# One table of single steps for the start of a pooled-attention and maxout kernel

## The chip, the cores and the metric

The kernel runs on one core of a Trainium2 chip. The metric is the device time of one execution in microseconds; a time given for a kernel is the median of several executions. The engines are named as in the profile: PE (TensorE), DVE (VectorE), ACT (ScalarE), POOL (GpSimd) and SP (SyncE, which here only issues transfers). Each executes its own instructions in the order in which the program gives them.

## The reference

Four batches of 12288 queries attend to 768 keys each. The keys are averages of 4x4 patches of `kv`, projected by `w_sr`, and they are the values too. The result, 49152 rows of 128, goes through a maxout layer with three matrices and an output matrix.

```python
kv_pool = kv.reshape(B, H // 4, 4, W // 4, 4, C).mean(axis=(2, 4))   # B=4, H=384, W=32, C=128
k = v = kv_pool.reshape(B, -1, C) @ w_sr                             # 768 keys for each batch
s = (1 / np.sqrt(C)) * (q @ k.transpose(0, 2, 1))                    # q: (4, 12288, 128)
a = np.exp(s - s.max(-1, keepdims=True))
a /= a.sum(-1, keepdims=True) + 1e-09
x = (a @ v).reshape(B * N, C)
h = np.maximum(np.maximum(x @ w1, x @ w2), x @ w3)                   # w: (128, 768), float64
out = (h @ w_out).astype(np.float32)                                 # w_out: (768, 128), float64
```

## The kernel before

The queries are cut into 96 groups (`NG`) of 512 rows, and a group into four tiles of 128. Nearly every matmul operand is split into two float16 parts, a high and a low one, scaled by powers of two, and three products of the parts stand for one. So for a group PE does:

- four score tiles (`scores`, token S): six matmuls of 128x384 each, into one of two double banks `ps_s`;
- the attention (`attend`, token X, in two halves of nine matmuls), from the softmax weights that a DMA transpose has turned into `aT`;
- six hidden blocks (`hidden`, token H): three matmuls of 128x512 for `w2 - w1` and three for `w3 - w1`, into the two banks `ps_h`. With `w1` taken off beforehand the maximum of three becomes a maximum with zero, and what `w1` itself adds comes back through one product of `w1` and `w_out` (`product_w1`, `w1o`);
- six projections (`project`, token O), three matmuls each and three more with `w1o` for the last block.

Around a score tile, DVE takes the maximum (`soft_max`, m, tiles `mx` and `nb`), ACT the exponential (`soft_exp`, e, tile `a`) and the cast to float16 (`soft_hi`, c), POOL the remainder (`soft_lo`, l, tile `ahl`), and SP issues the transpose to `aT`. Around a hidden block, ACT does a relu (R), DVE the maximum with the second product (M, tile `h`), ACT the cast (C, `hh`) and POOL the remainder (L, `hl`). `attended_hi` and `attended_lo` (xh, xl) split the attention's result; the q tokens load (qd), scale (qc), measure (qp), and split (qh, ql) the queries.

The order is written out by hand. A wrapper (`InOrder`) keeps each engine's instructions in the order of the program. From the first hidden block on, the strings of `ORDER`, twelve of them for the six blocks of an even and an odd group, say in which order the tokens' steps are issued. A token takes all that has come due (`drain`).

What stands before that is a straight list of calls. It loads `w_sr`, the twelve pieces of the first batch's `kv` (512 KB each) and the first queries; it sums the patches with DVE adds, folds and PE products with the identity (`gather`), projects and splits the keys; then come the weights. The weights arrive as 64-bit floats. `Weights64` makes a 32-bit float of each value: it clamps the upper word's magnitude (`clamp`), shifts it left by three (`shift`), adds three bits of the lower word (`low`) and the sign (`sign`); then `w1` is taken off (`rest`), the peak is found (`top`), and two float16 parts are made (`split_hi` on ACT, `split_lo` on DVE). Four matrices in two halves make eight such objects; their steps form a list `todo`, and `more(n)` issues the next n of them at chosen places, between the softmax steps of the groups 0 and 1 and, through `late`, between their hidden blocks. In the first half the clamp runs as an Abs on ACT and a max-min on POOL, in the others as a mask and a max-min on DVE. The buffers of `kvp`, 13 of 512 KB, hold both the pieces of `kv` and the raw weights.

Of the kernel before, what the change touches and what calls it, by code (L numbers as in the profile page):

```python
# [20 lines left out]
def kernel(  # L21
# [34 lines left out]
    R = 4  # L56
# [76 lines left out]
    col = const.tile([C, 1], F32, name="col")  # L133
    d_top = const.tile([P, 2, 4], F32, name="d_top")
# [15 lines left out]
    FIRST = (1, 1, 1, 1, 0, 1, 1, 1, 1, 2, 0, 1)  # L150
    LEFT = (12, 12, 12, 12, 12)
    LO_ON_DVE, HI_ON_DVE, HL_ON_DVE = ((), (6, 8), ())
    OUT_AT, OUT_ON = (1, 8), ("dve", "dve")
    ATTEND = {0: (4, 4), 1: (4, 4)}
    LATE = (1,)
    W_LOW, W_HIGH = 2.0 ** -15 * 1.125, 122879.9921875
# [15 lines left out]
    OUTS = {2: (), 3: (), 4: (0, 1, 2)}  # L172

    def sr_weights():
        e = prep.tile([C, C], F32, name="sr_e")
        dve.tensor_scalar(
            out=e.bitcast(I32), in0=wsr_sb.bitcast(I32), scalar1=0x7FFFFFFF, scalar2=None, op0=ALU.bitwise_and
        )
        ps = spare(True)
        mm(out=ps[:, :C], lhsT=ones, rhs=e, start=True, stop=True)  # L180
        pow2(col_row, ps[:, :C])
        dve.reciprocal(out=e, in_=col_row)
        dve.tensor_tensor(out=wsr_sb, in0=wsr_sb, in1=e, op=ALU.mult)
# [20 lines left out]
    class Weights64:  # L204
# [7 lines left out]
        def __init__(self, n, w, h, hi, lo, wide=False):  # L212
            self.n, self.h, self.wide, self.w = n, h, wide, w
            self.lay = (lambda t: t.rearrange("p (t c) -> p t c", c=C)) if wide else lambda t: t
            self.hi, self.lo = hi, lo
# [16 lines left out]
        def shift(self):  # L232
            dve.tensor_scalar(
                out=self.e.bitcast(I32), in0=self.e.bitcast(I32), scalar1=3, scalar2=0x3FFFFFF8,
# [18 lines left out]
        def rest(self, on=pool):  # L253
            on.tensor_tensor(out=self.e, in0=self.e, in1=W[0, self.h].e, op=ALU.subtract)
# [14 lines left out]
    def size_d(h):  # L269
        top = d_top[:, h]  # L270
        dve.tensor_reduce(out=top[:, 3:4], in_=top[:, :3], axis=AX.X, op=ALU.max)
        times(top[:, 3:4], top[:, 3:4], col)
        W["ps"] = spare(True)
        mm(out=W["ps"][:, :1], lhsT=ones, rhs=top[:, 3:4], start=True, stop=True)

    def sized_d(h):
        pow2(d_size[h], W.pop("ps")[:, :1], SMALL, LARGE)
# [46 lines left out]
    class Keys:  # L324


        def __init__(self, b):
# [3 lines left out]
            self.acc = {}  # L331
# [3 lines left out]
            self.top = tiny.tile([1, 1], F32, name="pool_top", bufs=2)  # L335
# [24 lines left out]
        def fold(self, s, i, n):  # L360

            view = self.pieces[s, i].rearrange("p (u j c) -> p u j c", u=KU, c=C)
            dve.tensor_tensor(out=view[:, :, :n], in0=view[:, :, :n], in1=view[:, :, n:2 * n], op=ALU.add)

        def gather(self, s, i, n, first, last):
# [4 lines left out]
            for u in range(KU):  # L370
# [13 lines left out]
        def gathered_size(self):  # L384
            self.turn_tops(True)
            self.tops()
            self.size(True)
            self.sized()

        def gathered_project(self, s):  # L390
            if s == 0:
                self.kps = (ps_x.tile([P, G], F32, name="ps_x"), ps_o.tile([P, NJ, C], F32, name="ps_o"))
            out = self.kps[1].rearrange("p j c -> p (j c)") if s == KS - 1 else self.kps[0][:, s * PW:]
# [5 lines left out]
        def gathered_hi(self, n):  # L399
            ps, ks = ((self.kps[0], slice(0, G)), (self.kps[1].rearrange("p j c -> p (j c)")[:, :PW], slice(G, NK)))[n]  # L400
            act.mul(out=self.k_hi[:, ks], in_=ps, mul=self.up)

        def gathered_lo(self, n):
            ps, ks = ((self.kps[0], slice(0, G)), (self.kps[1].rearrange("p j c -> p (j c)")[:, :PW], slice(G, NK)))[n]
# [26 lines left out]
        def turn_tops(self, first=False):  # L431
            self.tops_ps = spare(first)
            dve.tensor_reduce(out=self.m[:, KS:KS + 1], in_=self.m[:, :KS], axis=AX.X, op=ALU.max)
            mm(out=self.tops_ps[:1, :P], lhsT=self.m[:, KS:KS + 1], rhs=ident, start=True, stop=True)

        def tops(self):
            dve.tensor_reduce(out=self.top, in_=self.tops_ps[:1, :P], axis=AX.X, op=ALU.max)

        def size(self, first=False):
            self.size_ps = spare(first)  # L440
            mm(out=self.size_ps[:, :1], lhsT=ones[:1], rhs=self.top, start=True, stop=True)

        def sized(self):
            ps = self.size_ps[:, :1]
            dve.tensor_scalar(
                out=self.g.bitcast(I32), in0=ps.bitcast(I32), scalar1=EXPO, scalar2=None, op0=ALU.bitwise_and
# [24 lines left out]
        def values(self):  # L471
            sp_dma.dma_start_transpose(out=self.v_hi, in_=self.k_hi)
            sp_dma.dma_start_transpose(out=self.v_lo, in_=self.k_lo)
# [16 lines left out]
    def q_cols(g):  # L490
        t = q_half(g)
        pool.tensor_tensor(out=t, in0=t, in1=col_row.unsqueeze(1).to_broadcast([P, NJ, C]), op=ALU.mult)

    def q_peak(s):
# [3 lines left out]
        dve.tensor_reduce(out=row, in_=st["q"][s], axis=AX.XY, op=ALU.max, apply_absolute_value=True)  # L498
# [170 lines left out]
    def hidden_lo(g, f):  # L669
        h, hh = st["h"][g, f]  # L670
        hl = hp.tile([P, G], F16, name="hl", bufs=HB_)
        (dve if g * NFT + f in HL_ON_DVE else pool).tensor_tensor(out=hl, in0=h, in1=hh, op=ALU.subtract)
# [134 lines left out]
    def made(i, h, clamp_on=dve):  # L807
        w = W[i, h]
        return [lambda: w.clamp(clamp_on), w.shift, w.low, w.sign]

    def halves(h, clamp_on=dve, rest_on=pool):
        rests = [lambda i=i: W[i, h].rest(rest_on) for i in (1, 2)]
        return [
            *made(0, h, clamp_on), *made(1, h, clamp_on), rests[0], *made(2, h, clamp_on), rests[1],
            W[0, h].top, W[1, h].top, W[2, h].top, lambda: size_d(h),
        ]

    def splits(h):
        return [
            lambda: sized_d(h), W[1, h].split_hi, W[2, h].split_hi, W[1, h].split_lo, W[2, h].split_lo,  # L820
        ]

    first, second = halves(0, pool), halves(1)
    todo = [
        *first, *second[:2], *splits(0), *second[2:], *made(3, 0)[:2], *splits(1), *made(3, 0)[2:],
        W[3, 0].top, ratio_u, *made(3, 1), W[3, 1].top, size_u, sized_u,
        *(f for h in range(2) for f in (W[3, h].split_hi, W[3, h].split_lo)),
    ]

    def more(n):  # L830
        for _ in range(min(n, len(todo))):
            todo.pop(0)()

# [5 lines left out]
    k = KT[0] = Keys(0)  # L839
    for i in range(R):  # L840
        k.load(0, i)
    q_load(0)
    for s in range(1, KS):
        for i in range(R):
            k.load(s, i)

    sr_weights()
    k.gather(0, 0, R, True, False)
    k.gather(0, 1, R, False, False)
    k.add(0, 2, 3)  # L850
    k.gather(0, 2, R, False, True)
    q_cols(0)
    q_cols(1)
    k.gathered(0)
    q_peak(0)
    q_hi(0)
    q_hi(1)
    k.gather(1, 0, R, True, False)
    k.gathered_project(0)
    k.gathered_peak(0)  # L860
    k.add(1, 1, 2)
    q_lo(0)
    W[0, 0].load()
    q_lo(1)
    for w in ((1, 0), (2, 0), (0, 1), (1, 1), (2, 1), (3, 0), (3, 1)):
        W[w].load()
    k.gather(1, 1, R, False, False)
    k.gather(1, 3, R, False, True)
    k.gathered(1)
    k.add(2, 0, 1)  # L870
    k.fold(2, 0, 2)
    k.gather(2, 0, 2, True, False)
    k.gathered_peak(1)
    k.fold(2, 2, 2)
    k.gather(2, 2, 2, False, False)
    k.gathered_project(1)
    k.fold(2, 3, 2)
    k.fold(2, 3, 1)
    k.gather(2, 3, 1, False, True)
    k.gathered(2)  # L880
    more(1)
    k.gathered_peak(2)
    k.turn_tops(True)
    k.gathered_project(2)
    more(2)
    k.tops()
    k.size(True)
    more(2)
    k.sized()
    k.gathered_hi(0)  # L890
    k.gathered_hi(1)
# [247 lines left out]
```

## Time and profile before

| | us |
|---|---|
| median of 3 runs | 2051.13 |
| lowest and highest | 2050.55, 2052.91 |
| the profiled execution | 2051.95 |
| its span in the trace | 2050.2 |
| PE busy in the span | 1981.4 |
| DVE, ACT, POOL busy | 1505.8, 1453.6, 1414.8 |

The profile is of one execution. A line of the timeline gives start, duration, engine, source line (L103 is the wrapper's line, so steps are told apart by tile names), operation, tile written and tiles read, shape, and in brackets how long the engine had been idle and what ended that. A line of the groups gives count, busy time, mean duration in ns and the idle time before. Matmuls overlap in PE's pipeline, so a matmul's duration is longer than its share of PE's time; the distance between starts is the price.

### The profile page before, as it was taken

The numbers are of one execution on the slowest core, as the hardware profiler recorded it, in microseconds if no ns is written. First come the engines' busy times: TensorE is split into PE (matmuls) and PEld (weight loads), VectorE is DVE, ScalarE is ACT, GpSimd is POOL, SyncE is SP. The second block draws the span as 40 slices with busy tenths as digits, with TensorE's granted clock in tenths as the row PEclk, the third lists the DMA queues.
The fourth block names the chain that finished last, engine by engine and source line by source line (L and its number), as shares of the span: only waits on it lengthen the run. The fifth ranks groups of instructions, "written<-read, shape, count | busy, mean of one in ns | idle before, by whom it ended". The sixth has DMA issues, their size and how long they took to land.

```text
span 2050.2 us, 29146 instructions
## 1 busy us (share of the span) xinstructions
PE 1981.4 (97%) x9797; PEld 965.8 (47%) x9797; DVE 1505.8 (73%) x2471; ACT 1453.6 (71%) x2529; POOL 1414.8 (69%) x1068
## 2 busy tenths in 40 slices
PE   5599999999999999999999999999999999999998
PEld 4344444444444444444444444444444444444444
DVE  5758887777777887777777788677776777777775
ACT  3367777777777777777777777677777777777774
POOL 3357776777776677677777777777777777777764
PEclk8699999999999999999999999999999999999999
DMA  8268866767668866675667787666766665667662
GB/s 250 54 137 179 170 139 114 141 131 138 124 126 187 190 132 126 130 145 119 129 139 163 163 173 137 131 127 128 139 132 133 129 139 121 132 131 139 122 120 67
DMA packets 839960, 283.30 MB, mean 138 GB/s; under 512 B 813441, under 2 KB 814593, under 8 KB 839809
## 3 DMA queue, kind: packets, MB, share of 16 engines
q1 hardware_dynamic: 839808, 281.43, 67.2%
q8 instruction: 77, 1.26, 0.2%
q14 instruction: 75, 0.61, 0.1%
HBM read 53.54 MB, written 25.17 MB: 38 GB/s over the span
## 4 chain that ended last, share of the span: by engine, by line
PE 81%; DVE 7%; ACT 4%; DMA 4%; POOL 2%; issue 2%; SPq 0%; DVEq 0%; ACTq 0%; POOLq 0%
PE ps_h L103 31%; PE ps_o L103 18%; PE ps_x L103 17%; PE ps_s L103 15%; DMA aT<-ahl 3%; DVE h L103 1%; ACT ahl L103 1%; POOL ahl L103 1%; DVE w_e L103 1%; DVE q_row L103 1%; ACT a L103 1%; DVE mx L103 1%; ACT hh L103 1%; ACT xh L103 1%; DVE rs L103 1%
## 5 line engine op out<-in xcount | busy, mean ns | idle before, releaser
L103 POOL TENSOR_TENSOR ahl<-a,ahl 128x768 f16<-128x768 f32 x384 | 628.9, 1648 | 307.8 <-issue 188.1
L103 POOL TENSOR_TENSOR hl<-h,hh 128x512 f16<-128x512 f32 x575 | 670.4, 1176 | 191.8 <-ACT hh L103 191.4
L103 DVE SCALAR_TENSOR_TENSOR h<-ps_h,h 128x512 f32<-128x512 f32 x575 | 396.5, 690 | 185.8 <-ACT h L103 92.5
L103 ACT ACTIVATE h<-ps_h 128x512 f32<-128x512 f32 x575 | 341.7, 594 | 244.0 <-PE ps_h L103 240.5
L103 ACT CAST hh<-h 128x512 f16<-128x512 f32 x577 | 349.8, 615 | 170.1 <-DVE h L103 170.0
L103 DVE TENSOR_REDUCE mx<-ps_s 128x1 f32<-128x768 f32 x384 | 366.3, 954 | 108.6 <-PE ps_s L103 107.8
L103 PE MATMUL ps_h<-xh,d_hi 128*128 128x512 f16 x1150 | 437.3, 380 | 5.1 <-DVE h L103 2.7
L103 PE MATMUL ps_h<-xl,d_hi 128*128 128x512 f16 x1150 | 437.2, 380 | 2.9 <-DVE xl L103 2.9
L103 PE MATMUL ps_h<-xh,d_lo 128*128 128x512 f16 x1150 | 437.0, 380 | 0.0
L103 ACT ACTIVATE a<-ps_s,nb,q_sc 128x768 f32<-128x768 f32 x384 | 378.3, 987 | 66.5 <-DVE nb L103 60.4
L103 PE MATMUL ps_x<-aT,v_hi 128*128 128x512 f16 (+1 forms) x1188 | 376.4, 375 | 18.5 <-DMA aT<-ahl 16.7
L103 PE MATMUL ps_s<-k_hi,qT 128*128 128x384 f16 x1536 | 379.0, 329 | 10.6 <-ACT a L103 9.2
L103 PEld LDWEIGHTS <-d_hi 128*128 128x128 f16 x2308 | 226.3, 98 | 260.6 <-issue 6.5
L103 PE MATMUL ps_o<-hh,wo 128*128 128x512 f16 x1140 | 339.1, 379 | 0.0
L103 PEld LDWEIGHTS <-qT 128*128 128x128 f16 x2304 | 227.0, 99 | 203.6 <-issue 17.1
L103 ACT CAST ahl<-a 128x768 f16<-128x768 f32 x382 | 312.5, 832 | 4.5
L103 PEld LDWEIGHTS <-wo 128*128 128x128 f16 x1710 | 167.3, 98 | 191.9 <-issue 0.3
L103 PE MATMUL ps_s<-k_lo,qT 128*128 128x384 f16 x768 | 252.6, 329 | 0.0
L103 PE MATMUL ps_x<-aT,v_lo 128*128 128x512 f16 (+1 forms) x594 | 221.9, 375 | 0.0
L103 PE MATMUL ps_o<-hl,wo 128*128 128x512 f16 x570 | 216.1, 379 | 0.0
L103 POOL TENSOR_TENSOR q_sb<-q_sb,col_row 128x512 f32<-128x512 f32 x96 | 125.2, 1305 | 106.6 <-DMA q_sb<-in_q_dram 96.6
L103 PEld LDWEIGHTS <-v_hi 128*128 128x128 f16 x1188 | 116.5, 99 | 155.4 <-issue 13.1
(141 smaller groups left out, 1416.3 us busy)
## 6 DMA issues: line engine op xcount, KB each, us to landing
kv_piece<-in_kv_dram SPq DMA_DIRECT2D x48, 512.0 KB, 4.8
q_sb<-in_q_dram SPq DMA_DIRECT2D x48, 512.0 KB, 4.4
out_dram<-o_sb SPq DMA_DIRECT2D x95, 256.0 KB, 2.2
aT<-ahl SPq DMA_TRANSPOSE x384, 3.9
kv_piece<-in_moe_w_dram SPq DMA_DIRECT2D x6, 384.0 KB, 4.7
qT<-q_hl SPq DMA_TRANSPOSE x96, 3.4
o_turned<-o_planes SPq DMA_TRANSPOSE x95, 3.1
kv_piece<-in_moe_w_out_dram SPq DMA_DIRECT2D x2, 384.0 KB, 6.8
```

The lines of the kernel that those rows point to most:

```text
L103: return lambda **kw: tc.keep_in_program_order(op(**kw))
```

## The change

The straight list, the lists `FIRST`, `LEFT`, `ATTEND`, `OUTS` and `todo` with `more`, `softened` and `late` go. A table `START` of single steps replaces them: 23 rows, 318 tokens, which end where group 2 begins; the loop over `ORDER` starts at group 2. In the table each token issues one step (not all that is due), a dot adds arguments, and "!" puts the step on DVE instead of its usual engine (an `add` or `fold` on POOL instead). The new names: `wd`, `wm`, `ws`, `wl`, `wn`, `wr`, `wt`, `wh`, `wo` are load, scale, shift, low, sign, rest, top, split_hi and split_lo of weight i, half h; `kv` loads a piece, `gat` and `end` gather one; `value` turns one part of the keys into values; `dsize`, `dsized`, `usize`, `usized`, `ratio` make the weights' scales; `nk` is a step of the next batch's keys.

```diff
-        def clamp(self, on=dve):
+        def scale(self, on=None):
             self.e = wprep.tile([P, HALF_F], F32, name="w_e")
-            if on is pool:
-                act.activation(out=self.e, in_=self.r1.bitcast(F32), func=AF.Abs)
+            if on:
+                times(self.e, self.r1.bitcast(F32), W_DOWN)          # W_DOWN = 2.0 ** -112
             else:
-                dve.tensor_scalar(
-                    out=self.e.bitcast(I32), in0=self.r1, scalar1=0x7FFFFFFF, scalar2=None, op0=ALU.bitwise_and
-                )
-            on.tensor_scalar(
-                out=self.e, in0=self.e, scalar1=W_LOW, scalar2=W_HIGH, op0=ALU.max, op1=ALU.min
-            )
+                act.mul(out=self.e, in_=self.r1.bitcast(F32), mul=W_DOWN)
...
     def size_d(h):
         dve.tensor_reduce(out=top[:, 3:4], in_=top[:, :3], axis=AX.X, op=ALU.max)
-        times(top[:, 3:4], top[:, 3:4], col)
-        mm(out=W["ps"][:, :1], lhsT=ones, rhs=top[:, 3:4], start=True, stop=True)
+        mm(out=W["ps", h][:, :1], lhsT=col_ones, rhs=top[:, 3:4], start=True, stop=True)
...
         def turn_tops(self, first=False):
-            mm(out=self.tops_ps[:1, :P], lhsT=self.m[:, KS:KS + 1], rhs=ident, start=True, stop=True)
+            mm(
+                out=self.tops_ps[:, :P], lhsT=self.m[:, KS:KS + 1].to_broadcast([P, P]), rhs=ident,
+                start=True, stop=True,
+            )
         def tops(self):
-            dve.tensor_reduce(out=self.top, in_=self.tops_ps[:1, :P], axis=AX.X, op=ALU.max)
-        def size(self, first=False):
-            mm(out=self.size_ps[:, :1], lhsT=ones[:1], rhs=self.top, start=True, stop=True)
+            dve.tensor_reduce(out=self.g, in_=self.tops_ps[:, :P], axis=AX.X, op=ALU.max)
...
+    START = (
+        "wd.2.1 wm.2.1 sr qd qc! ws.2.1 wl.2.1 qc wd.0.0 qp qd wd.0.1 qh wm.0.1!",
+        "wd.2.0 ws.0.1 wm.2.0 qc! wn.2.1 ws.2.0 wm.0.0 qc wl.2.0 kv.2.1 kv.2.0 wn.2.0 add.2.0.1 fold.2.0.2",
+        "kv.2.3 ws.0.0 gat.2.0.2 wl.0.0 wn.0.0 fold.2.3.2.1 wr.2.0 wd.3.1 wd.3.0 kv.2.2 wm.3.1 ws.3.1 wl.3.1 turn_w1.0",
+        "kv.1.2 fold.2.2.2 wm.3.0 gat.2.2.2 wn.3.1 wl.0.1 kv.1.1 add.1.1.2 kv.0.0 gat.2.3.4.0 end.2.3.2.1 wd.1.1 wm.1.1 wn.0.1",
+        "wr.2.1 kv.1.0 gat.0.0.4 wt.3.1 ws.1.1 gathered_peak.2 kv.0.1 gat.1.0.4 gat.1.1.4 kv.0.2 wl.1.1 wd.1.0 kv.1.3 wm.1.0",
+        "qp wt.2.1 qh wn.1.1 ws.3.0 ws.1.0 wl.1.0 wn.1.0 gat.0.1.4 kv.0.3 add.0.2.3 end.1.3.4 ql gathered_peak.1",
+        "ql end.0.2.4 gathered.2 gathered.1 gathered_project.1 wr.1.0 gathered_peak.0 gathered.0 wt.0.1 turn_tops tops sized gathered_project.0 qe",
+        "gathered_hi.0 gathered_lo.0 gathered_project.2 gathered_hi.1 gathered_lo.1 S m S S qd wr.1.1 e c m",
+        "e c wt.1.0 wl.3.0 wt.1.1 m e wt.2.0 value.1 S m S dsize.1 wn.3.0",
+        "m S S c value.0 l X e e c! qh wt.0.0 l dsize.0",
+        "qe l l c l m m e e c dsized.0 wh.1.0 X X",
+        "ql dsized.1 ratio turn_w1.1 wt.3.0 wh.2.1 X wo.1.0 xh xl wh.2.0 c qc wo.2.0",
+        "S H S l m R wh.1.1 e M c S H qc C",
+        "l qp R m M l nk.1.1 wo.1.1 e H R S qh usize",
+        "M L wo.2.1 usized wh.3.0 H R m X c l M H wh.3.1",
+        "ql R X M C C C L e wo.3.0 wo.3.1 m L! product",
+        "c O xh xl H L R S M e c! H R M",
+        "C C O m l L e H R c! C O M S",
+        "S qe m qh H R O O M m e c! H e",
+        "C l L! S O R M C nk.1.4 l H X P.1.2 m",
+        "l c L C L R M e c C ql S H R",
+        "X m L e M O l l! c! L O S O xh",
+        "xl m L! qh C l O qd L ql",
+    )
...
-    for g in range(NG):
+    KT[0] = Keys(0)
+    for row in START:
+        for token in row.split():
+            start(token)
+    for g in range(2, NG):
```

More of the change, by code (lines that the diff above doesn't have):

```diff
@@ L358, in pool, with fold, gather @@
             )
[L360 to L365, printed above, removed]
+        def fold(self, s, i, n, on=dve, us=slice(None)):
+            view = self.pieces[s, i].rearrange("p (u j c) -> p u j c", u=KU, c=C)[:, us]
+            on.tensor_tensor(out=view[:, :, :n], in0=view[:, :, :n], in1=view[:, :, n:2 * n], op=ALU.add)
+        def gather(self, s, i, n, first, last, us=range(KU)):
             if first:
@@ L369, in gather @@
             piece = self.pieces[s, i].rearrange("p (u j c) -> p u j c", u=KU, c=C)
-            for u in range(KU):
+            for u in us:
                 for j in range(n):
@@ L382, in gathered_peak @@
             dve.tensor_reduce(out=self.m[:, s:s + 1], in_=ps, axis=AX.X, op=ALU.max, apply_absolute_value=True)
[L384 to L388, printed above, removed]
-        def gathered_project(self, s):
-            if s == 0:
-                self.kps = (ps_x.tile([P, G], F32, name="ps_x"), ps_o.tile([P, NJ, C], F32, name="ps_o"))
-            out = self.kps[1].rearrange("p j c -> p (j c)") if s == KS - 1 else self.kps[0][:, s * PW:]
+        def gathered_project(self, s):
+            if s == KS - 1:
+                self.kps[1] = ps_o.tile([P, NJ, C], F32, name="ps_o").rearrange("p j c -> p (j c)")
+            elif 0 not in self.kps:
+                self.kps[0] = ps_x.tile([P, G], F32, name="ps_x")
+            out = self.kps[1] if s == KS - 1 else self.kps[0][:, s * PW:]
             mm(
@@ L469, in projected, with value @@
             self.ps.pop(0)
[L471 to L473 removed]
+        def value(self, lo):
+            sp_dma.dma_start_transpose(out=(self.v_hi, self.v_lo)[lo], in_=(self.k_hi, self.k_lo)[lo])
     q_src = q.rearrange("b n c -> (b n) c").rearrange("(s p j) c -> s p j c", p=P, j=SJ)
@@ L805 @@
         W[3, h] = Weights64(3, moe_w_out, h, wo[h][:, :, 0], wo[h][:, :, 1], wide=True)
[L807 to L832, printed above, removed]
     sp_dma.dma_start(out=wsr_sb, in_=w_sr)
@@ L838 @@
     act.activation(out=warm, in_=ones[:, :1], func=AF.Exp)
[L839 to L891, printed above, removed]
-    more(1)
-    k.gathered_lo(0)
-    k.gathered_lo(1)
-    k.values()
-    q_exps(0)
-    q_load(1)
-    scores(0, 0)
-    scores(0, 1)
-    more(2)
-    def softened(g, j, n, then=None):
-        soft_max(g, j)
-        soft_exp(g, j)
-        soft_split(g, j)
-        if then:
-            scores(*then)
-        more(n)
@@ L934 @@
-    tiles = [(g, j) for g in range(1, NG) for j in range(NJ)][2:]
+    tiles = [(g, j) for g in range(NG) for j in range(NJ)]
+    products = [(0, j) for j in range(NJ)] + [(g, part) for g in range(1, NG) for part in range(2)]
     to_max, to_exp, to_hi, to_lo, to_merge, to_scale = [], [], [], [], [], []
-    to_relu, to_h, to_hh, to_hl = [], [], [], []
-    next_q = {"load": 3, "cols": 4, "peak": 2, "hi": 4, "lo": 4}
+    to_relu, to_h, to_hh, to_hl, to_xh, to_xl = [], [], [], [], list(range(NG)), []
@@ L938 @@
+    to_hidden, to_project = ([(g, f) for g in range(NG) for f in range(NFT)] for _ in range(2))
+    next_q = {"load": 0, "cols": 0, "peak": 0, "exps": 0, "hi": 0, "lo": 0}
     nxt = None
@@ L945, in turn, with some, step @@
         return n
-    def drain(queue):
-        while queue:
+    def some(queue, one):
+        for _ in range(1 if one else len(queue)):
             yield queue.pop(0)
-    def step(token, g, f):
-        n = g * NFT + f
+    def step(token, g, f, one=False, on=None):
         if token == "H":
-            hidden(g, f)
-            to_relu.append((g, f))
+            gf = to_hidden.pop(0)
+            hidden(*gf)
+            to_relu.append(gf)
         elif token == "R":
-            for gf in drain(to_relu):
+            for gf in some(to_relu, one):
                 to_h.append((gf, hidden_first()))
         elif token == "M":
-            for gf, h1 in drain(to_h):
+            for gf, h1 in some(to_h, one):
                 st["h"][gf] = hidden_max(h1)
@@ L964, in step @@
         elif token == "C":
-            for gf in drain(to_hh):
+            for gf in some(to_hh, one):
                 hidden_hi(*gf)
@@ L968, in step @@
         elif token == "L":
-            for gf in drain(to_hl):
-                hidden_lo(*gf)
+            for gf in some(to_hl, one):
+                hidden_lo(*gf, on)
         elif token == "O":
-            if g < 2:
-                late(n)
-            for m in OUTS.get(n, (n - 2,)):
-                if m >= 0:
-                    project(*divmod(m, NFT))
+            project(*to_project.pop(0))
         elif token == "S":
-            for _ in range(FIRST[n] if g < 2 else f not in (1, 4)):
-                if tiles:
-                    to_max.append(tiles.pop(0))
-                    scores(*to_max[-1])
+            if (one or f not in (1, 4)) and tiles:
+                to_max.append(tiles.pop(0))
+                scores(*to_max[-1])
         elif token == "X":
-            for part, slot in enumerate(ATTEND.get(g, (1, 4))):
-                if f == slot and g < NG - 1:
-                    attend(g + 1, part)
+            if (one or f in (1, 4)) and products:
+                g, part = products.pop(0)
+                (attend if g else attend_tile)(g, part)
         elif token == "m":
-            for t in drain(to_max):
+            for t in some(to_max, one):
                 soft_max(*t)
@@ L990, in step @@
         elif token == "e":
-            for t in drain(to_exp):
+            for t in some(to_exp, one):
                 soft_exp(*t)
@@ L1017, in step @@
             else:
-                for m in drain(to_scale):
+                for m in some(to_scale, one):
                     scale_out(m, finish_scale(m))
@@ L1025, in step @@
             q = turn("cols", NG)
-            if q:
-                q_cols(q)
+            if q is not None:
+                q_cols(q, on)
         elif token == "qp":
             s = turn("peak", NG // 2)
-            if s:
-                q_peak(s)
+            if s is not None:
+                q_peak(s, bool(on))
+            if not one:
+                step("qe", g, f)
+        elif token == "qe":
+            s = turn("exps", NG // 2)
+            if s is not None:
                 q_exps(s)
@@ L1044, in step, with start @@
             raise ValueError(token)
+    def start(token):
+        nonlocal nxt
+        k, on = KT[0], dve if token[-1] == "!" else None
+        name, *n = token.rstrip("!").split(".")
+        n = [int(x) for x in n]
+        both = {"": slice(None), 0: slice(0, 1), 1: slice(1, 2)}
+        if name == "sr":
+            sr_weights()
+        elif name == "kv":
+            k.load(*n)
+        elif name == "add":
+            k.add(*n[:3], on=pool if on else dve, us=both[n[3] if n[3:] else ""])
+        elif name == "fold":
+            k.fold(*n[:3], on=pool if on else dve, us=both[n[3] if n[3:] else ""])
+        elif name == "gat":
+            s, i, width, *u = n
+            k.gather(s, i, width, not k.begun.get(s), False, us=u or range(KU))
+            k.begun[s] = True
+        elif name == "end":
+            s, i, width, *u = n
+            k.gather(s, i, width, False, True, us=u or range(KU))
+        elif name in ("gathered", "gathered_peak", "gathered_project", "gathered_hi", "gathered_lo", "value"):
+            getattr(k, name)(*n)
+        elif name == "turn_tops":
+            k.turn_tops(True)
+        elif name in ("tops", "sized"):
+            getattr(k, name)()
+        elif name[0] == "w" and name[1:] in WEIGHTS:
+            getattr(W[n[0], n[1]], WEIGHTS[name[1:]])(*([on] if on else []))
+        elif name in AIDS:
+            AIDS[name](*n)
+        elif name == "nk":
+            r, f = n
+            if nxt is None:
+                nxt = Keys(1)
+            keys_step(r, f)
+        else:
+            step(name, *(n or (1, 0)), one=True, on=on)
+    WEIGHTS = {
+        "d": "load", "m": "scale", "s": "shift", "l": "low", "n": "sign", "r": "rest", "t": "top",
+        "h": "split_hi", "o": "split_lo", "z": "signs",
+    }
+    AIDS = {
+        "dsize": size_d, "dsized": sized_d, "ratio": ratio_u, "usize": size_u, "usized": sized_u,
+        "turn_w1": turn_w1, "product": product_w1,
+    }
     def keys_step(g, f):
@@ L1104 @@
     last_hidden()
-    project(NG - 1, NFT - 3)
-    project(NG - 1, NFT - 2)
-    project(NG - 1, NFT - 1)
+    for f in range(NFT - 3, NFT):
+        project(NG - 1, f)
     last_finish(NG - 1, rs)
```

138 lines of the change are left out of this document (59 added, 79 removed).

## The prediction

> **What bounds the kernel now.** I read the page's busy totals first, then busy time by stretch, then the timeline of the stretch that differs.
>
> ```profile
> PE 1981.4 (97%) x9797; PEld 965.8 (47%) x9797; DVE 1505.8 (73%) x2471; ACT 1453.6 (71%) x2529; POOL 1414.8 (69%) x1068
> ```
> ```profile
> 0.00:59.67 59.67, 35.51 (x240) 28.13 (x241) 34.00 (x69) 19.31 (x33) 21.21 (x21) 0.86 0.79 235
> 59.67:108.15 48.48, 27.70 (x94) 12.38 (x93) 33.10 (x71) 14.58 (x27) 16.60 (x13) 0.68 0.23 44
> 108.15:135.83 27.68, 26.95 (x140) 13.62 (x139) 17.53 (x30) 20.87 (x37) 16.83 (x13) 1.00 0.64 129
> 135.83:2050.20 1914.37, 1891.23 (x9327) 911.71 (x9325) 1421.12 (x2303) 1398.86 (x2432) 1360.18 (x1023) 1.00 0.68 138
> ```
>
> TensorE (PE) is busy 97% and is the bound, except at the start. The columns of the second fence are stretch, length, then busy time of PE, PEld, DVE, ACT, POOL, granted clock, DMA share and GB/s. I cut at hidden blocks ("H"): 59.67 us is the first H of group 0, 108.15 the sixth, 135.83 the thirteenth, which opens group 2. From there PE is busy 1891.23 of 1914.37 us, and the diff leaves that order of steps as it was. Whatever is won or lost therefore lies before 135.83. There, 135.83 us hold two groups that cost about 20 us each later, and between 59.67 and 108.15 DVE is the busiest engine (33.10 of 48.48), PE gets 27.70 at a granted clock of 0.68, and only five H are issued.
>
> The state at the end of the new table equals the state at 135.83: 12 H, 17 score tiles, 16 softmax splits, attention of groups 0 to 2, 10 projections. So the forecast is one question: at what time does the thirteenth H start?
>
> **Prices.** One PE stretch gives PE's; the groups of the first 120 us (busy, mean ns) give the others.
>
> ```profile
> 112.40 0.38 PE L103 MATMUL ps_h<-xh,d_hi 128*128 128x512 f16 x1
> 113.70 0.59 PE L103 MATMUL ps_o<-hh,wo 128*128 128x512 f16 x2
> 114.35 0.49 PE L103 MATMUL ps_s<-k_hi,qT 128*128 128x384 f16 x2
> 115.32 0.38 PE L103 MATMUL ps_h<-xh,d_hi 128*128 128x512 f16 x1
> 143.42 0.39 PE L103 MATMUL ps_x<-aT,v_hi 128*128 128x512 f16 x1 [1.92 <-DMA aT<-ahl]
> 145.37 0.38 PE L103 MATMUL ps_h<-xh,d_hi 128*128 128x512 f16 x1
> ```
> ```profile
> L103 POOL TENSOR_TENSOR ahl<-a,ahl 128x768 f16<-128x768 f32 x11 | 18.4, 1679 | 27.3 <-issue 19.5 <-ACT ahl L103 7.8
> L103 ACT ACTIVATE a<-ps_s,nb,q_sc 128x768 f32<-128x768 f32 x12 | 11.9, 988 | 17.9 <-DVE nb L103 17.9
> L103 DVE TENSOR_REDUCE mx<-ps_s 128x1 f32<-128x768 f32 x12 | 11.4, 951 | 1.2 <-PE ps_s L103 1.2
> L103 DVE SCALAR_TENSOR_TENSOR w_e<-kv_piece,w_e 128x384 int32<-128x384 int32 x16 | 8.9, 555 | 0.4
> L103 DVE TENSOR_SCALAR w_e<-w_e 128x384 int32<-128x384 int32 x8 | 5.9, 736 | 6.0 <-POOL w_e L103 5.8
> L103 DVE SCALAR_TENSOR_TENSOR h<-ps_h,h 128x512 f32<-128x512 f32 x8 | 5.5, 686 | 4.0 <-PE ps_h L103 2.0 <-ACT h L103 1.9
> L103 POOL TENSOR_SCALAR w_e<-w_e 128x384 f32<-128x384 f32 x3 | 4.4, 1488 | 11.7 <-ACT w_e L103 11.7
> L103 DVE TENSOR_SCALAR w_e<-w_e 128x384 f32<-128x384 f32 x5 | 4.3, 852 | 0.2
> L103 DVE TENSOR_SCALAR w_e<-kv_piece 128x384 int32<-128x384 int32 x5 | 1.9, 382 | 0.0
> L103 ACT ACTIVATE w_e<-kv_piece 128x384 f32<-128x384 f32 x3 | 1.6, 546 | 0.7 <-DMA kv_piece<-in_moe_w_dram 0.7
> L103 DVE TENSOR_TENSOR kv_piece<-kv_piece 128x1024 f32<-128x1024 f32 x3 | 3.7, 1224 | 4.8 <-DMA kv_piece<-in_kv_dram 4.8
> L103 DVE TENSOR_REDUCE d_top<-w_e 128x1 f32<-128x384 f32 x6 | 3.1, 548 | 2.5 <-POOL w_e L103 2.5
> L103 DVE SCALAR_TENSOR_TENSOR q_hl<-q_sb,q_up,q_hl 128x512 f16<-128x512 f32 x4 | 3.1, 808 | 2.0 <-ACT q_hl L103 2.0
> L103 DVE TENSOR_SCALAR nb<-mx,q_sc 128x1 f32<-128x1 f32 x12 | 2.6, 214 | 0.4
> ```
> ```profile
> 65.77 0.35 DVE L103 TENSOR_SCALAR w_e<-w_e 128x384 int32<-128x384 int32 x1
> 78.22 1.15 DVE L103 SCALAR_TENSOR_TENSOR d_lo<-w_e,d_up,d_hi 128x384 f16<-128x384 f32 x2 [0.74 <-ACT d_hi L103]
> 83.60 0.56 DVE L103 CAST ahl<-a 128x768 f16<-128x768 f32 x1 [0.55 <-ACT a L103]
> ```
>
> PE: an H is 113.70-112.40 = 1.30, a projection O 0.65, a score tile S 0.97, half an attention X 1.95. On DVE a shift that nothing holds up is 0.35, a low split 0.57, a cast 0.56.
>
> **The weights.** Eight half-matrices. The clamps cost 5x0.382 (mask) + 5x0.852 (max, min) = 6.2 us on DVE, 3x1.488 = 4.5 us on POOL, 3x0.546 on ACT. Now seven ACT multiplies at the Abs' 0.55 = 3.9 us and one DVE multiply at about 0.36. Shift, low bits and sign stay. Net: DVE -5.8, POOL -4.5, ACT +2.2 us; ACT is the least loaded of the two that trade (14.58 of 48.48), so I cost its 2.2 at nothing; without that cover it is 2.2. Work moved onto DVE by the table's "!" eats it again: two q scalings (about 0.7), five casts (0.56), three hidden and one softmax remainder (0.7, 1.0) = 7.3 us, against two casts before (1.1). DVE's total is therefore about unchanged (+0.4): removing clamps alone does not shorten the start, the reordering must.
>
> **The key and weight scales.** The reduced peak is broadcast by one matmul instead of two in a row, with one PE hop fewer on the keys' path; the two half weights' scales lose a 0.21 us multiply each and gain one of about 0.23. Together under 1 us on the path, and for the three later batches a tiny matmul pair each, between nothing and an O's 0.65 apiece off PE, in all at most 2. I take 1 on the path and nothing later.
>
> **The loads.** Now weights come among the keys' pieces, and two q loads stand ahead of most pieces; the last piece (0,3) is behind 8 weights, 11 pieces and 2 q. In MB of the sizes below: 12x0.524 + 8x0.393 + 2x0.524 (q, a piece's size) + 0.07 = 10.6.
>
> ```profile
> kv_piece<-in_kv_dram SPq DMA_DIRECT2D x48, 512.0 KB, 4.8
> kv_piece<-in_moe_w_dram SPq DMA_DIRECT2D x6, 384.0 KB, 4.7
> aT<-ahl SPq DMA_TRANSPOSE x384, 3.9
> 0.00:20.00 20.00, 14.35 (x95) 13.60 (x96) 8.96 (x17) 3.19 (x5) 3.20 (x8) 1.00 0.89 340
> 23.96 0.61 PE L103 MATMUL ps_s<-ident,kv_piece 128*128 128x128 f32 x4
> 29.72 0.69 ACT L103 ACTIVATE k_hi<-ps_x,k_up 128x512 f16<-128x512 f32 x1 [3.09 <-DVE g_exp L103]
> 30.46 0.80 PE L103 MATMUL ps_s<-k_hi,qT 128*128 128x384 f16 x2 [1.36 <-ACT k_hi L103]
> ```
>
> At 340 GB/s that is 31 us. Sync's queue is in order, and only 13 buffers hold pieces and raw weights, so from the 14th load on each waits for an old buffer: piece (0,1) for the sign step of weight (0,1), with four loads and the last piece behind it. By the DVE rows ahead of that step (17.5 us from 2.6 on, with waits for data) I put it at 22, before the queue runs dry. Then the chain that took 29.72-23.96 = 5.8 from the last gather to k_hi, plus one add of 1.2 and less the removed hop: first scores at 31+1.2+5 = 37, **6.5 us later than now** (30.46). That is what the change pays. Sync's transposes of q (two) come after the last load, those of v (two) ahead of the first tile's aT; at 3.9 to land and with nothing else queued I cost them at nothing, each 1.2 us of queue if an aT stood behind one. Bounds: DVE's rows 1 to 7 sum to 29.8 (weight steps 12.8, keys' adds, folds and peaks 6.8, q 6.6, scales 3.6), so 33 if it never waited; at its present share (34.00/59.67 = 0.57), 52.
>
> **First H.** From the first maximum at 38.3, DVE does 17.4 us in the table's rows 8 to 12: seven maxima at 0.95+0.21, five weight peaks at 0.55, two low splits, a low and a sign step, a q remainder of 0.81, a cast, scales and xl. It is all needed, mostly in this order, before the fourth tile is attended. 55.7 with no wait, 68.8 at the share 0.57; I take 4 us of waits: **59.7, the same time as now**. The difference is what is behind it: now 8 instead of 6 tiles scored, and of the weights' some 24 us of DVE work four low splits and the last scale are left (in the trace now only one half of three matrices is done by then).
>
> **From first to thirteenth H.** PE: 9 S 8.7, 12 H 15.6, 4 X 7.8, 11 O-sized products 7.2, the product of w1 and w_out 1.3 = 40.6 us at full clock. DVE's rows 13 to 23 sum to 36.1, ACT's to 34.8, POOL's to 28.5, so PE leads. Lower bound 40.6; upper 36.1 over DVE's present share of the slow stretch (33.10/48.48 = 0.68) = 53. To 40.6 I add 3 for a slow clock after the idle start, and 3.5 for DVE and POOL holding each other up:
>
> ```profile
> 102.81 0.58 PE L103 MATMUL ps_x<-aT,v_hi 128*128 128x512 f16 x1 [4.70 <-DMA aT<-ahl]
> 105.99 0.59 PE L103 MATMUL ps_x<-aT,v_hi 128*128 128x512 f16 x2
> 41.98 1.78 DVE L103 TENSOR_SCALAR w_e<-w_e 128x384 int32<-128x384 int32 x1 [4.44 <-POOL w_e L103]
> 41.91 1.64 POOL L103 TENSOR_TENSOR ahl<-a,ahl 128x768 f16<-128x768 f32 x1
> 59.18 1.63 DVE L103 SCALAR_TENSOR_TENSOR d_lo<-w_e,d_up,d_hi 128x384 f16<-128x384 f32 x1 [2.09 <-ACT d_hi L103]
> ```
>
> After 4.70 us idle, PE needs until 105.99 to reach full pace, 3.2 us. A shift beside POOL's remainder lasts 1.78 and ends with it, where a free one lasts about 0.36; a low split lasts 1.63 instead of 0.57. Fifteen such DVE steps stand in rows 13 to 23 (splits, casts, remainders, q); each could lose up to 1.2, POOL is busy some 60% of the time, and a wait that begins midway is half: 15x0.6x0.5x1.2 = 5, part of it in DVE's slack. So 47, close to the present pace of the last stretch (27.68 for seven H with 26.4 us of PE work), taken because DVE's weight work is gone from both.
>
> The Trainium skill ("SBUF — State Buffer", section "Who interferes with whom") says that a DVE instruction with two SBUF inputs or in a two-port mode and a GpSimd one that reads SBUF lock each other out for a whole instruction. That speaks against handing DVE the casts and remainders: if every one of the fifteen met a full POOL remainder, the estimate by that rule is 15x1.2 = 18 us in place of 3.5, 2037 instead of 2023. The trace agrees with the lock (1.78 beside 1.64), not with its always hitting.
>
> **Sum.** 59.7+47 = 106.7 against 135.83: 29 us less. The rest is untouched, its 1.92 us wait at 141.5 too. The profiled execution took 2051.95 (span 2050.2, 1.75 around it), 0.8 over the median 2051.13. 2051.95-29 = **2023**, 1.4% faster.
>
> **Rivals.**
> 1. *DVE idles as it does now.* First scores at 45, halfway to their bound, and pace by the 0.68 share: H at 45+1.3+17.4+4 = 68, +53 = 121, 15 us gained, 2037. For it: DVE waits for POOL 5.8 us (shift row above) and others now; against: rows 2 to 7 keep independent work between a step and its reader. Chance 0.13.
> 2. *No change.* All upper bounds together: first scores 52, first H 52+1.3+17.4/0.57 = 84, +53 = 137: 2053. The change would then only move the waiting. Chance 0.05.
> 3. *Slower: the ring of two ps_h buffers.* An H may start only when ACT's relu and DVE's max of the one before have freed both buffers; those stand in order behind maxima that wait for scores, which wait in PE's order behind that H's predecessors. It decides at a mean pace over 76.2/12 = 6.35 us per H (135.83-59.67 = 76.2). In the present slow stretch it is 48.48/5 = 9.7. At 7 per H: 59.7+84 = 144, 2060. Against: what slowed those five were weight steps between the maxima, now nearly gone. Chance 0.09.
> 4. *The clamps alone are the gain, the order gives nothing*: at most DVE's 5.8 + 1 for the scales: 2045. Inside rival 1's side; chance 0.03.
>
> **How the numbers follow.** Forecast 0.70, in 2011 to 2034 by itself. 0.2% (4 us) is about what a measurement can tell. Faster 0.70+0.13+0.03 = 0.86, same 0.05, slower 0.09. The range 2010 to 2042 reaches down to first H at 55.7, 40.6 and the clock's 3 (2015), less some 4 for loads faster than 340 GB/s, and takes in rival 1 with its spread; rivals 2, 3 and 4 stay out.
>
> **What would show it.** In the profile after: last kv piece landing near 31 and first scores 35 to 40; ACT rows w_e x7 near 0.55; no POOL w_e tensor_scalar; first H within 56 to 65; thirteenth H near 107, with H spaced about 4 us; granted clock about 1 from 65 on; the stretch after it again about 1914 us. I am wrong if the thirteenth H starts after 125, if Sync's loads stall in mid-table, or if H spacing stays above 6.

## The result, and the profile after

The changed kernel takes 2018.91 us (median of 4 runs, 2017.68 to 2023.50) against 2051.61 for the kernel before in the same set: ratio 0.9844, interval 0.9827 to 0.9861, so 1.6% faster; 2023 had been forecast. The profiled execution took 2023.50 us, the slowest of the four, with a span of 2021.7.

First the page's totals of the changed kernel, then its busy time by stretch, cut where the prediction cut: first scores at 39.24 us, first hidden block at 59.05, thirteenth at 105.77.

```profile
PE 1971.2 (98%) x9797; PEld 963.3 (48%) x9797; DVE 1503.6 (74%) x2469; ACT 1454.0 (72%) x2530; POOL 1406.7 (70%) x1059
```
```profile
0.00:39.24 39.24, 21.74 (x140) 20.26 (x140) 30.24 (x65) 8.63 (x17) 8.87 (x12) 1.00 0.82 289
39.24:59.05 19.81, 13.57 (x127) 9.45 (x127) 17.11 (x40) 14.33 (x26) 13.09 (x8) 1.00 0.80 143
59.05:105.77 46.72, 43.50 (x213) 21.31 (x211) 37.63 (x64) 31.76 (x58) 26.00 (x18) 0.96 0.68 121
105.77:2021.70 1915.93, 1892.38 (x9321) 912.31 (x9319) 1418.65 (x2303) 1399.24 (x2431) 1358.71 (x1021) 1.00 0.69 138
```

The columns are length, busy time of PE, PEld, DVE, ACT and POOL with their instructions, granted clock of PE, DMA share and GB/s. The last row hardly differs from that of before (1914.37 us, PE busy 1891.23). The gain lies above it: 135.83-105.77 = 30.1 us in this execution, whose rest is 1.6 longer. The third row shows where: PE is now busy 43.50 of 46.72 us at a granted clock of 0.96, where the old stretch of five hidden blocks had 27.70 of 48.48 at 0.68. The first row says where the weights' work went. Up to its first scores the kernel before used DVE for half of the time, and the same view of it, cut there, shows it:

```profile
0.00:30.46 30.46, 20.11 (x131) 18.20 (x132) 15.35 (x36) 5.67 (x11) 6.14 (x10) 0.95 0.96 337
```

Now DVE does 30.24 us of work in 39.24, while the transfers run. PE's timeline after, at the first scores, the first hidden block, the one long wait, and the thirteenth block:

```profile
39.24 0.48 PE L103 MATMUL ps_s<-k_hi,qT 128*128 128x384 f16 x2 [0.87 <-ACT k_hi L103]
59.05 0.38 PE L103 MATMUL ps_h<-xh,d_hi 128*128 128x512 f16 x1
79.47 0.38 PE L103 MATMUL ps_h<-xh,d_hi 128*128 128x512 f16 x1 [2.46 <-DVE w1o L103]
105.77 0.38 PE L103 MATMUL ps_h<-xh,d_hi 128*128 128x512 f16 x1
```

### The profile page after: what moved, and what is told of

Read it like the earlier page. It is cut to its first block, busy times and chain, and to the rows that moved or that the text cites. A ratio compares the mean times of both kernels' runs of the same rounds, so it can differ in the third digit from the quotient of the medians.

```text
span 2021.7 us, 29151 instructions
## 1 busy us (share of the span) xinstructions
PE 1971.2 (98%) x9797; PEld 963.3 (48%) x9797; DVE 1503.6 (74%) x2469; ACT 1454.0 (72%) x2530; POOL 1406.7 (70%) x1059
## 4 chain that ended last, share of the span: by engine, by line
PE 80%; DVE 7%; DMA 5%; ACT 4%; issue 2%; POOL 2%; SPq 0%; DVEq 0%; ACTq 0%; POOLq 0%
PE ps_h L103 31%; PE ps_o L103 17%; PE ps_x L103 17%; PE ps_s L103 15%; DMA aT<-ahl 4%; DVE h L103 1%; POOL ahl L103 1%; DVE q_row L103 1%; ACT ahl L103 1%; ACT a L103 1%; DVE mx L103 1%; ACT xh L103 1%; ACT hh L103 1%; ACT h L103 1%; DVE rs L103 1%
```

## The experiments

The marks used below are the starts of the first scores, the first H and the thirteenth H in each trace. Three sets were run, each beside the kernel before (2053.22, 2052.70 and 2053.76 us).

### The base, repeated

> The changed kernel once more, as the base of this set. Theory A (the start holds the whole gain): first scores near 39.2, first H near 59, thirteenth H near 106 us again, and the rest of the span the same 1914 to 1916 us; the median near 2019. If the first profile's later part (1915.9 against 1914.4) was a chance delay, this trace's rest is nearer 1911 to 1914.

2020.90 us, ratio 0.9842 (0.9827 to 0.9856). First scores 37.68, first H 59.26, thirteenth 104.29, the rest 1914.0 us, where the two cases of the expectation meet. Theory A's marks hold within 1.7 us. The first scores come 1.6 us earlier, and yet the first H does not. From the first scores to the first H, PE's granted clock was 0.84 here, and 1.00 in the first trace:

```profile
37.68:59.26 21.58, 16.46 (x128) 10.71 (x128) 17.03 (x40) 14.47 (x26) 12.56 (x8) 0.84 0.79 147
```

So a mark of a single trace can move by nearly 2 us (21.58 against 19.81) with the kernel unchanged.

### The clamps alone, in both orders

```diff
# after_clamps: the changed kernel, scale() as clamp() was
-                act.mul(out=self.e, in_=self.r1.bitcast(F32), mul=W_DOWN)
+            on = dve if on or self.wide or self.h else pool
...          # then Abs on ACT or the mask on DVE, the max-min, and the old masks of shift and sign
# before_scale: the kernel before, clamp() as scale() is
...
+            act.mul(out=self.e, in_=self.r1.bitcast(F32), mul=2.0 ** -112)
```

> The changed kernel with the old clamps put back in the place of the multiply (first halves of w1, w2, w3: Abs on ACT and max-min on POOL; the other five: mask and max-min on DVE), the table as it is. Theory A (the order is the gain; clamps are 6 us of DVE work, partly under the loads): 1 to 7 us slower than the changed kernel, 2020 to 2026. Rival B (the clamps are the gain): it falls back by 20 us or more, 2039 to 2050.

> The kernel before, its order untouched, with ACT's multiply in the place of all eight clamps. Theory A: DVE loses 6.2 us and POOL 4.5 of work in a stretch where DVE sets the pace, so 3 to 9 us faster, 2042 to 2048. Rival B: most of the 32 us is here already, 2020 to 2030.

With the clamps back, the changed kernel takes 2027.47 us, ratio 0.9869 (0.9853 to 0.9886): 6.6 over the base's 2020.90. Without them, the kernel before takes 2046.60, ratio 0.9965 (0.9952 to 0.9978): 6.6 less. So the order with the clamps left in brings 2053.22-2027.47 = 25.8 us, the whole is 2053.22-2020.90 = 32.3, and the clamps come to about 6.6 in either order. That size is rough: the four runs of after_clamps go from 2024.66 to 2034.64, and its interval just meets the base's. The 25.8 hold the changed scales of keys and weights too, which the prediction put at 1 us and no run separates. Rival B is out. PE's timeline of after_clamps, then of before_scale:

```profile
43.08 0.48 PE L103 MATMUL ps_s<-k_hi,qT 128*128 128x384 f16 x2 [0.87 <-ACT k_hi L103]
64.33 0.38 PE L103 MATMUL ps_h<-xh,d_hi 128*128 128x512 f16 x1
111.19 0.38 PE L103 MATMUL ps_h<-xh,d_hi 128*128 128x512 f16 x1
```
```profile
53.72 0.38 PE L103 MATMUL ps_h<-xh,d_hi 128*128 128x512 f16 x1 [0.69 <-ACT xh L103]
97.76 0.38 PE L103 MATMUL ps_h<-xh,d_hi 128*128 128x512 f16 x1
125.30 0.38 PE L103 MATMUL ps_h<-xh,d_hi 128*128 128x512 f16 x1
```

In the new order the clamps cost 4 to 5 us ahead of the first scores already (43.08) and nothing after the first H (46.9 us to the thirteenth, as without). DVE's fold of an early piece shows why, for PE's long run of gathers (the matmuls that sum the patches) begins behind it. In the changed kernel it starts at 19.25, in after_clamps at 24.35, both times without a wait for data, so it is DVE that is late:

```profile
19.25 0.68 DVE L103 TENSOR_TENSOR kv_piece<-kv_piece 128x512 f32<-128x512 f32 x1
```
```profile
24.35 0.68 DVE L103 TENSOR_TENSOR kv_piece<-kv_piece 128x512 f32<-128x512 f32 x1
```

In the old order their removal brings the first H 6 us earlier and saves 4 more up to the sixth.

### Weight steps where they are free and where they are not

```diff
# before_thin and after_thin
         def low(self):
-            dve.scalar_tensor_tensor(...)
+            pass
         def sign(self):
-            dve.scalar_tensor_tensor(...)
+            pass
```

> The kernel before without the weights' low-bits and sign steps (16 DVE steps of 0.555, 8.9 us; the weights lose three bits and their signs). Theory A (in the old start weight steps on DVE between the maxima set the pace of the hidden blocks): the thirteenth H 8 us or more earlier than 135.8, 2041 to 2046. Rival E (the ring of ps_h buffers or something else sets the pace): 0 to 4 us.

> The changed kernel without the same 16 steps. Theory A (the table has put them under the loads, where DVE's time is free): 14 of the 16 stand ahead of the first scores, so first scores at most 1 us earlier and the whole 0 to 3 us faster than the changed kernel, less than half of what the same cut brings to the kernel before. Rival D (DVE sets the start in both): 7 to 9 us faster here too.

The same 16 DVE steps bring the kernel before 2052.70-2045.85 = 6.9 us, ratio 0.9968 (0.9957 to 0.9979), and the changed kernel nothing: 2021.33, ratio 0.9855 (0.9840 to 0.9869), its base 0.9838 to 0.9842 in the other sets. Both kernels then leave out three bits and the sign of each weight, and nothing else. PE's timeline of before_thin (first, sixth and thirteenth H), then of after_thin (first scores, first and thirteenth H, and DVE's fold of the early piece):

```profile
58.41 0.38 PE L103 MATMUL ps_h<-xh,d_hi 128*128 128x512 f16 x1 [1.07 <-ACT xh L103]
101.51 0.38 PE L103 MATMUL ps_h<-xh,d_hi 128*128 128x512 f16 x1
128.91 0.38 PE L103 MATMUL ps_h<-xh,d_hi 128*128 128x512 f16 x1
```
```profile
37.84 0.49 PE L103 MATMUL ps_s<-k_hi,qT 128*128 128x384 f16 x2 [0.87 <-ACT k_hi L103]
57.43 0.38 PE L103 MATMUL ps_h<-xh,d_hi 128*128 128x512 f16 x1
104.16 0.38 PE L103 MATMUL ps_h<-xh,d_hi 128*128 128x512 f16 x1
17.93 0.69 DVE L103 TENSOR_TENSOR kv_piece<-kv_piece 128x512 f32<-128x512 f32 x1 [1.17 <-DMA kv_piece<-in_kv_dram]
```

In the old order most of the saving appears between the first and the sixth H (48.5 to 43.1 us), where 10 of the 16 steps stood: about their own 5.5 us. Eight of the ten do not stand between maxima, as I had put it: DVE has no maximum from 56.4 to 81.2 us. They stand ahead of the weights' peaks, from which the scales are made, and for these PE waited longest in that stretch:

```profile
75.87 0.56 PE L103 MATMUL ps_h<-d_top,ones 128*128 128x1 f32 x2 [6.91 <-DVE d_top L103]
```

The saving is 6.9 and not the 8 that I had asked of theory A, but well above rival E's 4. Without the steps this wait is still 6.17 us and the stretch 43.1, so the 16 steps are a small part of what made it slow. In the new order 8.9 us less DVE work leaves the first scores where they were (37.84 against 37.68 to 39.24): the fold comes 1.3 us earlier and has then waited 1.17 us for its data, and PE's gathers behind it take as long as before (15.83 us against 15.93). With the clamps gone, DVE is little behind the loads there, and more cuts buy next to nothing.

### Fewer loads

```diff
# after_10pieces, in START
-    kv.0.1 ... gat.1.1.4 ... kv.1.3 ... gat.0.1.4 ... end.1.3.4
+    ... end.1.1.4 ...
```

> The changed kernel without two of the first batch's twelve pieces: (0,1) and (1,3) are neither loaded nor summed, so the first keys lack two of every sixteen rows of a patch sum. 1.05 MB less before the last piece, which lands 2.6 us earlier at 400 GB/s. Theory A (loads set the time of the first scores, and the first scores set all behind them): first scores near 36.6, first H near 56.5, thirteenth H 2 to 3 us earlier, 2016 to 2019. Rival D (DVE's weight steps set them anyway): first scores within 1 us of 39.2 and the time unchanged.

```profile
36.20 0.48 PE L103 MATMUL ps_s<-k_hi,qT 128*128 128x384 f16 x2 [0.87 <-ACT k_hi L103]
54.72 0.38 PE L103 MATMUL ps_h<-xh,d_hi 128*128 128x512 f16 x1
100.49 0.38 PE L103 MATMUL ps_h<-xh,d_hi 128*128 128x512 f16 x1
```

The first scores come 1.5 to 3.0 us earlier than in the base's traces of the first profile and the first set, the thirteenth H 3.8 to 5.3. That looks like theory A, but the run does not show it. The two pieces take their gathers with them, 32 of 124, some 3.5 us of PE at the pace of 92 in 10 us; the gathers begin at 19.82 as in the base (19.47 to 19.99), and only their run is shorter. Loads or gathers, the run cannot tell, and the base's trace speaks for the gathers (next section). Nor is all of the gain at the later marks due to the pieces: in this trace the granted clock is 1.00 from the first scores to the thirteenth H, while a slow clock cost each of those two 1.7 to 1.8 us (46.72 against 45.03 us from the first H on, 21.58 against 19.81 ahead of it). The time does not settle it: the median is 2018.91, ratio 0.9843 (0.9828 to 0.9858), not to be told from the base's; the profiled execution took 2016.14, the other three 2018.8 to 2019.9.

### The steps moved to DVE, and one swapped pair

```diff
# after_usual: "!" taken off c, l, L and qc
# after_swap
-        "ql R X M C C C L e wo.3.0 wo.3.1 m L! product",
+        "ql R X M C C C L e wo.3.0 wo.3.1 m product L!",
# after_mix: the swap, and "!" taken off l and L alone
```

> The changed kernel with the sign for DVE taken off its two q scalings, five casts, three hidden remainders and one softmax remainder, so that they run on POOL and ACT as usual. Theory A (moving them balances the engines): ACT gains 4 us of casts and POOL 7.7 us of remainders and scalings in the start, 1 to 6 us slower than the changed kernel. Rival C (DVE and POOL hold each other up, so the moves cost more than they bring): 1 to 6 us faster.

> The changed kernel with one pair of tokens swapped, 'L! product' to 'product L!': the low part of w1's product no longer waits on DVE behind a hidden remainder (2.06 us in the trace) and frees its ps_h bank earlier. Theory A (every wait of PE between first and thirteenth H counts): the 2.5 us wait of the sixth H goes, thirteenth H 1 to 2.5 us earlier. Rival F (the ring has slack behind it): the remainder is late instead and the thirteenth H within 0.5 us of 105.8.

> The changed kernel, unaltered, as the base for the three beside it: 2018 to 2021, ratio to before 0.984.

> All of the table's steps on their usual engines again, with more rounds. In its first trace the thirteenth H came 2.1 us earlier than in the changed kernel's of the same set, while the medians were 0.4 us apart. Theory G (what the moves to DVE bring and what they lose beside POOL cancel): within 2 us of the base. Rival C (the moves cost): 2 to 4 us faster than the base.

> The swapped pair again, with more rounds. In its first trace the wait for w1o was gone and the thirteenth H stood 2.3 us earlier than in the changed kernel's. Theory A: the median follows, 1 to 3 us faster than the base. Rival F (it is lost again behind, or drowned in the waits for aT): within 1 us.

> Swap, and the three hidden remainders and the softmax remainder back on POOL; the five casts and two q scalings stay on DVE. A candidate for a better version: if the w1o wait and the long DVE remainders (2.06 us) are what is left of PE's waits, thirteenth H at 100 to 102 and 2 to 4 us faster than the base. If POOL becomes late instead (its share of the stretch rises from 26 to 30 of 46 us), no gain.

| kernel | us | ratio to before | thirteenth H |
|---|---|---|---|
| base, set 3 | 2019.65 | 0.9838 (0.9825 to 0.9851) | 105.29 |
| after_usual, sets 1, 3 | 2021.29, 2021.50 | 0.9844, 0.9846 (0.9832 to 0.9859) | 102.18, 102.09 |
| after_swap, sets 2, 3 | 2019.45, 2019.74 | 0.9845, 0.9840 (0.9826 to 0.9853) | 101.98, 103.99 |
| after_mix, set 3 | 2017.54 | 0.9827 (0.9814 to 0.9841) | 102.14 |

Putting the moved steps back on their usual engines changes the time by no more than a measurement can tell, although the thirteenth H comes 2 to 3 us earlier in both traces. The moves to DVE are worth nothing here (theory G). The wait for w1o is gone in every kernel of the table but the base, and again only the trace shows it, not the median: rival F's "drowned" for the swap. For after_usual the traces show where the lead goes: its rest is 1916.7 and 1917.1 us, with PE waiting 26.3 and 26.5, against 1912.9 to 1915.9 and 21.8 to 23.6 in the base's three. after_mix is the fastest, 2.1 us below its base, but the intervals overlap; it is a candidate, not a shown gain. The wait as it stands in the changed kernel, from DVE's and POOL's timelines:

```profile
77.09 2.06 DVE L103 TENSOR_TENSOR hl<-h,hh 128x512 f16<-128x512 f32 x1
79.08 0.34 DVE L103 SCALAR_TENSOR_TENSOR w1o<-ps_h,w1o_up,w1o 128x128 f16<-128x128 f32 x1
76.97 1.64 POOL L103 TENSOR_TENSOR ahl<-a,ahl 128x768 f16<-128x768 f32 x1 [1.32 <-DVE mx L103]
```

The remainder hl, 0.68 us elsewhere on DVE, starts beside a POOL remainder and ends 0.5 us after it; w1o stands behind it on DVE, and PE behind w1o for 2.46 us.

## Why the prediction was right

- **The question.** It rested on one mark, the thirteenth H: 106.7 forecast, 105.77, 104.29 and 105.29 measured, from 135.83. Since the other stretch is unchanged but for a scatter of a few us, the sum followed. The medians gained 32.3 to 34.1 and not 29; one trace of before against three of after can't tell whether the rest lies in the start or behind it.
- **First scores.** Forecast 37, measured 37.68 to 39.24. The last piece was summed from 30.38 us on, near the forecast 31 for its landing, but the loads were not what the scores waited for. I had 6.2 us from the landing to the scores; it was 8.9, because PE, for whose gathers the sum has no term, was busy with those of older pieces without a break from 19.99 to 35.92. The projections and scales come behind them, and DVE's peaks of the pooled keys wait for PE twice 0.7 us:

```profile
19.99 4.64 PE L103 MATMUL ps_s<-ident,kv_piece 128*128 128x128 f32 x20 [1.32 <-DVE kv_piece L103]
24.42 11.49 PE L103 MATMUL ps_h<-ident,kv_piece 128*128 128x128 f32 x96
19.99:35.92 15.93, 15.93 (x117) 15.93 (x118) 12.54 (x22) 2.36 (x5) 3.94 (x3) 1.00 0.68 251
```
```profile
30.38 1.67 DVE L103 TENSOR_TENSOR kv_piece<-kv_piece 128x1024 f32<-128x1024 f32 x1 [0.48 <-DMA kv_piece<-in_kv_dram]
31.98 1.48 DVE L103 SCALAR_TENSOR_TENSOR q_hl<-q_sb,q_up,q_hl 128x512 f16<-128x512 f32 x1
34.16 0.42 DVE L103 TENSOR_REDUCE pool_max<-ps_h 128x1 f32<-128x256 f32 x1 [0.71 <-PE ps_h L103]
35.95 0.42 DVE L103 TENSOR_REDUCE pool_max<-ps_h 128x1 f32<-128x256 f32 x1 [0.70 <-PE ps_h L103]
```

In the repeated run the gathers begin at 19.47 and take 14.89 us: that is the 1.6 us by which its scores come earlier. The forecast of this mark was near for the wrong reason.

- **First H.** Forecast 59.7, measured 59.05, but by two errors that cancel: the scores 2 us later, and 18.2 us from the first maximum (40.87) to the first H instead of 21.4. DVE was busy 17.11 of the 19.81 us after the first scores, so the 4 us that I gave for waits were too many. In the repeated run the scores came at 37.68, and a slow clock (0.84) on the way took the gain: 59.26. That the mark agrees so closely is in part luck.
- **First to thirteenth H.** Forecast 47, measured 46.72, 45.03 and 46.72. PE's work plus its slow clock came to 43.50 (40.6+3 forecast) and its waits to 3.2, of which 2.46 is the wait for w1o behind a remainder beside POOL, the kind that I had priced at 3.5. The clock's 3 was mis-sized and misplaced: after the idle start it was 1.00, and it fell only after the wait for w1o. Where it did not fall (45.03), PE was busy 41.81 us, so the slow clock cost 1.7 and the work 1.2 more than the sum.
- **The clamps.** This term failed. "Removing clamps alone does not shorten the start" is refuted by before_scale. I set the saving of 5.8 us on DVE against 6.2 us moved onto DVE and called them even: DVE's busy time before the thirteenth H did stay (34.00+33.10+17.53 = 84.6 before, 30.24+17.11+37.63 = 85.0 after), yet the clamps are worth 6.6 us in both orders and the moved steps nothing in either direction. An engine's sum over the whole start was the wrong measure: in the changed order the clamps stand ahead of the first scores, and the fold that PE's gathers wait for comes 5 us later with them (24.35 against 19.25); the moved steps stand mostly behind the first H, where PE is (43.50 of 46.72 us). In the old order the clamps' removal brings the first scores forward by 2.3 us (28.20), the first H by 6 and the sixth by 10.
- **The order.** "The reordering must" is shown: 25.8 of the 32 us, by after_clamps. That weight steps on DVE were on the path of the old start and hardly are on that of the new one is shown by the thin pair, for the 16 steps that it takes out. What the table's other part brings, the finer order of the groups 0 and 1, no run separates from the weights' new places. Rivals 1 and 2 did not occur; rival 3's pace was 3.9 us per H against the deciding 6.35, the ring waiting once, for w1o.
- **DVE beside POOL.** Forecast 3.5 us of net loss in the last stretch. The remainder hl at 2.06 us shows it, and after_usual bounds it: taking eleven steps off DVE moved the time by nothing and the thirteenth H by 2 to 3 us, of which 1.7 to 1.8 are a slow clock that each of the base's traces shows in the start and neither of after_usual's does.

## What to carry to other kernels

While the first data is still coming in, the in-order engines are free, and whatever does not depend on the late data belongs there: ask of each engine what it could already do, and load for that first even if the main path starts later. Price a removed step by the stretch in which it stands and by what the path waits for there, not by the engine's sum: the same 9 us of DVE work were worth 7 us in one order and nothing in the other. A few microseconds gained at a mark in one trace need not show in the median: look at the granted clock up to the mark, and at the waits behind it.

## What the runs showed of the hardware

A wait of PE can cost more than itself. At the same place of two executions of the changed kernel, PE waited 2.5 us for a transposed tile in the first and 1.6 in the second; these are the two 7 us stretches, the first kernel trace and then the repeated one:

```profile
681.00:688.00 7.00, 4.47 (x22) 1.97 (x21) 6.75 (x9) 5.08 (x9) 2.73 (x3) 0.99 1.20 246
688.00:695.00 7.00, 7.00 (x29) 3.04 (x28) 2.95 (x6) 2.19 (x4) 4.21 (x4) 0.77 0.12 42
```
```profile
681.00:688.00 7.00, 5.42 (x26) 2.33 (x25) 5.36 (x8) 5.18 (x10) 4.17 (x4) 1.00 1.01 231
688.00:695.00 7.00, 7.00 (x37) 3.47 (x36) 5.65 (x9) 5.21 (x9) 5.92 (x5) 1.00 0.20 49
```

After the longer wait the granted clock is 0.77 in the next 7 us and 29 matmuls were done instead of 37; the group stores of the first trace, 0.6 us behind those of the repeated one up to there, are 3.2 us behind from there on: 0.9 us more wait cost 2.6. But the length of the wait alone does not decide. The wait for w1o lasts 2.46 us in all six traces that have it; in four of them the clock is 0.76 in the 7 us behind it, in the other two (after_again, after_10pieces) 1.00. And in before_scale a wait of 1.96 us for aT, ending at 132.93, was enough, where 1.92 in the kernel before (from 141.5 on) was not. First the 7 us behind the w1o wait in the first trace, then in the repeated one, then 3.5 us behind before_scale's wait:

```profile
79.47:86.47 7.00, 7.00 (x27) 3.06 (x27) 3.47 (x6) 1.87 (x4) 1.93 (x2) 0.76 0.29 56
```
```profile
79.67:86.67 7.00, 7.00 (x37) 3.55 (x37) 4.29 (x8) 3.55 (x7) 2.86 (x3) 1.00 0.29 56
```
```profile
133.60:137.10 3.50, 3.50 (x10) 1.30 (x9) 0.99 (x1) 0.04 (x1) 0.44 (x1) 0.52 0.83 161
```

The Trainium skill ("TensorE: Matmul & The Clock Gate", section "What's actually happening") says that PE falls to half rate after an idle window of about 3.4 us, counted in windows that run freely. The traces agree on half rate (0.52 above), and one wait with two outcomes fits windows that run freely; but waits of 1.96 to 2.53 us, shorter than 3.4, were enough here. I had taken the rest of the span as fixed; over all traces it was 1912.6 to 1923.1 us. The longest is before_scale's, whose lead at its 28th store, 7.8 us, had shrunk to 1.8 in the span:

```profile
125.30:2048.40 1923.10, 1894.91 (x9328) 912.84 (x9325) 1422.12 (x2302) 1400.10 (x2432) 1359.26 (x1023) 1.00 0.69 137
```

PE waited 28.2 us there (1923.10-1894.91) against 23.1 in the kernel before, and was busy 3.7 us longer for the same work. The granted clock accounts for the 3.7: before_scale's rest has two such slow stretches, behind waits for aT of 1.96 and 2.26 us, and that of the kernel before has none. The other traces bear this out: PE is busy 1890.3 to 1891.6 us in a rest without a slow stretch (nine traces), 1892.4 to 1893.0 with one (three) and 1896.7 with four (after_clamps), 1.4 to 2 us for each. The other 5.1 us of before_scale's are longer waits, and why these differ is open.
